# Sparse attention and two mixtures of experts on one core: drains, branch hints and fillers moved in the second mixture

## The chip, the cores and the metric

The kernel runs on one NeuronCore of a Trainium2 chip. The metric is the device time of one execution in microseconds (us), smaller is better. Three executions of the kernel before took 527.5, 528.46 and 528.85 us (median 528.46); one more was profiled and took 526.34 us.

## The reference

Three stages follow each other. Inputs are float32: 1152 tokens (2 batches of 576), width 512, eight experts of inner width 1024 in both mixtures, capacity 288 in the second.

```python
attn = softmax(mask(scale * q @ k.T)) @ v          # half the heads local, half strided
x = rows(attn)                                     # (1152, 512)

# first mixture: two experts a token, chosen by noisy logits
noisy = x @ w_gate + log1p(exp(x @ w_noise)) * noise
for each token, for its 2 best experts e, weight g:
    out[t] += g * (relu(x[t] @ w1[e]) @ w2[e])

# second mixture, on that output: one expert a token, 288 rows an expert at most
logits = x @ w_gate2;  e = argmax(logits);  g = softmax(logits)[e]
out[t] = g * (relu(x[t] @ v1[e]) @ v2[e])
```

## The kernel before, in words

The order of the work on each engine is written out by hand. PE (TensorE) multiplies; ACT and DVE empty PSUM and split float32 weights into a high part `hi` (ACT, or POOL by a CAST at L75) and a rest `lo` (DVE, L82), so that a product is three matmuls (`hi`·x high, `hi`·x low, `lo`·x high); SP loads the weights in pieces of 512 KB into six buffers `raw`; POOL issues the indirect transfers that gather and scatter rows. Three stages matter here.

**The second routing** (from L861). DVE finds the best expert of each token, PE counts ranks (L377 to L382), and `early_list(0, ...)` builds the row list of expert 0: for each of nine token tiles DVE compares (`hot`, L429) and PE sums (`place`, L435), then DVE writes the list (L439) and POOL gathers expert 0's first 128 rows (`gather`, L403). DVE then works out `bits`, a number that tells for each expert whether it has more than 128 and more than 256 rows, and all engines load it into a register (`values_load`, L900). After that PE does some matmuls whose result nobody reads (`warm`, L122; called fillers here), the second list (with a filler of 256 columns behind each of the first four tiles), and in the middle of it the four transposes of expert 0's rows (`x_cols`, L409). POOL meanwhile scatters the full list to DRAM (L500) and reads it back as `lst` (L509).

**The second mixture** (from L1061), experts 0 to 7. A pass takes 128 rows of an expert (the third one 32): `block` runs eight steps of three matmuls for the first product (two halves of four steps), then eight steps for the second. Expert e always runs `first_block`. A second and a third pass stand in `other_blocks` behind branches (`tc.If`, L1051 and L1059) that the flags decide. A branch that is taken jumps over the pass to a short stretch in which each engine raises the semaphores that the skipped instructions would have raised (EVENT_SEMAPHORE, on POOL also INC_SWDGE_SEM). In this run experts 0, 3, 5 and 6 skip both further passes, 1, 4 and 7 skip the third, and 2 runs all three.

`tell(e, b)` puts a hint on a branch into the stream of every engine: one or two register operations (L906) and a BRANCH_PREFETCH_HINT (listed at the last line of the kernel function's caller, L1166). Before, `tell(e, 1)` stands ahead of `first_block(e)` and `tell(e, 2)` at the start of the second pass.

`also(at)` is called by `block` at fixed places and holds the side work: weight splits, the transposes of the next rows, `last_rows` (the output of the expert before), `rows_ahead` (POOL gathers for the expert after next) and, at place 6, `pool.drain()` (L1032), on which POOL waits. Expert 1 at place "between" decodes `lst` on DVE (L513 to L516) and lets POOL gather expert 2's rows into the buffer that the trace calls `hot`.

Another `pool.drain()` stands in `finish` of the first mixture (L761).

```python
    def early_list(e, rk, ix, limit, busy=0, hook=None, q=1):

        for c in range(NT):
            early_hot(e, rk, limit, [c])
            early_place(c, limit)
            warm(bank[6], busy, q)
```

Of the kernel before, what the change touches and what calls it, by code (L numbers as in the profile page):

```python
# [38 lines left out]
def blocks(n):  # L39
    return [(a, min(128, n - a)) for a in range(0, n, 128)]  # L40
# [3 lines left out]
def attention_moe_moe_kernel(ctx: ExitStack, tc: tile.TileContext, a, out, capacity):  # L44
    nc = tc.nc
    pe, act, dve, pool, sp = nc.tensor, nc.scalar, nc.vector, nc.gpsimd, nc.sync
# [38 lines left out]
    def split(eng=None):  # L85
        split_lo(split_hi(), eng or dve)
# [32 lines left out]
    def warm(ps, n, q=4):  # L119

        for _ in range(n):
            pe.matmul(ps.rearrange("p (a b) -> p a b", a=4)[:, :q], ones,  # L122
                      ones[:, None, :].to_broadcast([128, q, 128]), start=True, stop=True)
# [219 lines left out]
    bank = [banks[:, i] for i in range(8)]  # L343
# [10 lines left out]
    def small(name, shape=(128, NT, E), dt=F32):  # L354
        return rt.tile(list(shape), dt, name=name)
# [18 lines left out]
    def count_ranks(sb, first, last):  # L374

        ps = bank[7][:, :(NT + 1) * E].rearrange("p (c e) -> p c e", e=E)
        pe.matmul(ps[:, :NT, :], tri, sb, start=first, stop=False, skip_group_check=True)  # L377
        pe.matmul(ps[:, NT, :], ones, sb[:, NT - 1, :], start=False, stop=False,
                  skip_group_check=True)
        for c in range(NT - 1):  # L380
            n = NT - c
            pe.matmul(ps[:, c + 1:NT + 1, :], ones, sb[:, c, None, :].to_broadcast([128, n, E]),  # L382
                      start=False, stop=last and c == NT - 2, skip_group_check=True)
        return ps

    def ranks(ps, chosen, tag):


        pen = small("pen" + tag)
        dve.tensor_scalar(pen, chosen, -BIG, BIG, op0=OP.mult, op1=OP.add)  # L390
        rk = small("rk" + tag)
        dve.tensor_tensor(rk, ps[:, :NT, :], pen, op=OP.add)
        at = small("rank" + tag)
        act.activation(at, ps[:, :NT], AF.Copy, scale=24.0)
        cnt = small("cnt" + tag, (128, E))
        act.copy(cnt, ps[:, NT])
        return rk, at, cnt
# [27 lines left out]
    def early_hot(e, rk, limit, cs=range(NT)):  # L425

        for c in cs:
            n = min(limit, 128 * (c + 1))
            dve.tensor_scalar(hot[:, c, :n], count[:, :n], rk[:, c, e:e + 1], None, op0=OP.is_equal)  # L429

    def early_place(c, limit):

        ps = bank[7][:, :3]
        for b, (s0, m) in enumerate(blocks(min(limit, 128 * (c + 1)))):
            pe.matmul(ps[:, b:b + 1], hot[:, c, s0:s0 + 128], place[:, c:c + 1],  # L435
                      start=c == 0 and b == 0, stop=c == NT - 1, skip_group_check=True)

    def early_index(ix):
        dve.tensor_scalar(ix, bank[7][:, :3], float(T), None, op0=OP.add)  # L439
# [7 lines that stand above are left out]
            if c == 6 and hook:  # L447
                hook()
        early_index(ix)
# [74 lines left out]
    def by_turns(*chains):  # L524

        chains = list(chains)
        while chains:
            chains = [c for c in chains if next(c, c) is not c]
# [330 lines left out]
    c2 = min(capacity, C1)  # L859
    nb2 = blocks(c2)  # L860
# [4 lines left out]
    rk3, at3, cnt3 = ranks(count_ranks(ohb3, True, True), oh3[:, 0], "3")  # L865
# [3 lines left out]
    h = yT.rearrange("p d s -> p (d s)")[:, :FF]  # L869
    L2 = Lists("2", oh3, at3, c2)  # L870
    early2 = [small(f"early2{i}", (128, 3), I32) for i in range(2)]
    early_list(0, rk3, early2[0], c2)
    gather(xg[0], acc, early2[0], c2, (0,))
    act.activation(d3, d3, AF.Exp)
    g3 = small("g3", (128, 1, NT))
# [2 lines left out]
    def weights2():  # L878
        dve.tensor_reduce(m3, d3, axis=AX.X, op=OP.add)
        yield  # L880
        dve.tensor_scalar(m3, m3, 1.0e-9, None, op0=OP.add)
        yield
        dve.reciprocal(g3[:, 0], m3)
        yield
        L2.weights(g3)

    def bits2():

        f = [small(f"bits{i}", (128, E)) for i in range(2)]
        for i in range(2):  # L890
            dve.scalar_tensor_tensor(f[i], cnt3, 128.0 * (i + 1), four_e, op0=OP.is_gt, op1=OP.mult)
            yield
        dve.scalar_tensor_tensor(f[0], f[1], 2.0, f[0], op0=OP.mult, op1=OP.add)
        yield
        dve.tensor_reduce(f[1][:, :1], f[0], axis=AX.X, op=OP.add)
        yield
        dve.tensor_copy(bits, f[1][:, :1])

    by_turns(weights2(), bits2(), L2.places())
    more_blocks = nc.values_load(bits[0:1, 0:1], engines=engines, min_val=0, max_val=4 ** E - 1)  # L900

    def has(e, b):
        return (more_blocks >> (2 * e + b - 1)) & 1

    def tell(e, b):
        tc.mark_branch_hint_location(f"block{e}_{b}", hint=has(e, b), engines=engines)  # L906

    pending = [split_hi() for _ in range(2)]
    early_hot(1, rk3, c2)
    warm(bank[6], 5)  # L910
    for c in range(NT):
        early_place(c, c2)
        if c < 4:
# [66 lines left out]
    def first_block(e):  # L980
        def two(n=2):
            for _ in range(n):
                if e == 0 and pending:
                    split_lo(pending.pop(0), dve)
                else:
                    split()

        def last_rows():
            put_rows(e - 1, 0, bank[0] if e % 2 else bank[7])

        def rows_ahead():
            if e + 2 < E:
                gather(xg[(e + 2) % 3], acc, L2.ix[:, e + 2], c2)

        def next_turn():
            s.append(x_turn(xg[(e + 1) % 3], 0, nb2[0][1], bank[6]))

        def also(at):
            if at == "start":
                if e:  # L1000
                    two()
                if e > 1:
                    last_rows()
                    rows_ahead()
            elif at == "up":
                if e:
                    two(1)
            elif at == "between":
                if e == 1:
                    L2.decode()  # L1010
                    gather(xg[2], acc, L2.ix[:, 2], c2)
                if e:
                    two(1)
                if len(nb2) > 1:
                    s.append(x_turn(xg[e % 3], 1, nb2[1][1], bank[5]))
                if e != 1 and e + 1 < E:
                    next_turn()
            elif at == 2:
                if len(nb2) > 1:
                    x_split(s[0], xs2, 128, nb2[1][1])  # L1020
                if e != 1 and e + 1 < E:
                    x_split(s[-1], xs2, 0, nb2[0][1])
            elif at in (3, 4, 5, 6) and e + 1 < E:
                if e == 1 and at == 6:
                    next_turn()
                    x_split(s[-1], xs2, 0, nb2[0][1])
                if e and at % 2 == 0:
                    split_lo(split_hi(on_pool=True), dve)
                else:
                    two(1)  # L1030
                if at == 6:
                    pool.drain()  # L1032
                if e == 1 and at == 4:
                    last_rows()
                if e == 1 and at == 6:
                    rows_ahead()
            elif at == 6:
                pool.drain()

        s = []  # L1040
        block(e, 0, bank[7] if e % 2 else bank[0], also)

    def other_blocks(e):

        def also(at):
            if at == "between" and len(nb2) > 2:
                x_cols(xg[e % 3], xs2, 2, nb2[2][1], ps=bank[6])

        if len(nb2) == 1:
            return  # L1050
        with tc.If(has(e, 1) > 0, preferred_fallthrough_block=True, label=f"block{e}_1"):  # L1051
            if len(nb2) > 2:
                tell(e, 2)
            if e == 0:
                L2.decode()
            block(e, 1, bank[5], also)
            put_rows(e, 1, bank[5])
            if len(nb2) > 2:
                with tc.If(has(e, 2) > 0, preferred_fallthrough_block=True, label=f"block{e}_2"):  # L1059
                    block(e, 2, bank[6], lambda at: None)  # L1060
                    put_rows(e, 2, bank[6])  # L1061

    put = []
    for e in range(E):
        if len(nb2) > 1:
            tell(e, 1)
        first_block(e)
        if e == E - 1:
            put_rows(e, 0, bank[7])
        other_blocks(e)  # L1070
# [99 lines left out]
```

## Time and profile before

| what | value |
|---|---|
| three executions | 527.5, 528.46, 528.85 us |
| profiled execution, its time | 526.34 us |
| its span, first to last instruction | 524.2 us |
| PE busy (matmuls) | 493.6 us, 94% |
| DVE, ACT, POOL busy | 300.7, 259.7, 190.0 us |
| mean granted TensorE clock | 0.974 |
| HBM traffic | 85.93 MB read, 16.26 MB written |
| second routing and second mixture | about 326 to 524 us of the span |

All times of the trace count from the first instruction. "Idle before" a row is the time that its engine stood still ahead of it, and behind the arrow stands what ended that time; an engine's name with a q is its instruction queue. [...] The profiled execution has 2.1 us outside its span.

### The profile page before, as it was taken

The page shows a single profiled execution, that of the slowest core. Times are in us where ns is not written, and L with a number is a line of the kernel's source. Part 1 is how long each engine was busy: PE and PEld are TensorE (multiplying, and loading weights), DVE is VectorE, ACT ScalarE, POOL GpSimd, SP SyncE. Part 2 cuts the span into 40 slices and gives each one's busy share as a digit, 9 for nine tenths or more (in the row PEclk, how much of TensorE's full clock was granted, in tenths as well). Part 3 has the DMA queues.
Part 4 walks back from the last instruction along what each step waited for, and adds up shares of the span by engine and source line. Part 5 has one row for each costly group of instructions (what it writes and reads, how often), then busy time and mean ns, then how long its engine had stood idle before and what let it go on. Part 6 is the DMA issues. An engine that isn't in the chain of part 4 may idle for free. (4 is left out here: it accounts for less than half of the span.)

```text
span 524.2 us, 9702 instructions
## 1 busy us (share of the span) xinstructions
PE 493.6 (94%) x3446; PEld 420.7 (80%) x3446; DVE 300.7 (57%) x664; ACT 259.7 (50%) x512; POOL 190.0 (36%) x233
## 2 busy tenths in 40 slices
PE   9999679999999999999999999797899999999896
PEld 4776559999999999999999998475677577777684
DVE  3997749565464555546555463655446048648731
ACT  4886617453544536454453532345254166457531
POOL 1444068853232150323203042682642055143300
PEclk9999859999999999999999999799999999999899
DMA  8975758789767686765747375338747049848600
GB/s 245 257 185 161 264 177 273 221 287 319 237 163 220 215 200 230 175 198 138 215 158 173 128 180 135 69 112 269 275 169 254 20 157 320 295 145 282 241 21 1
DMA packets 35742, 102.04 MB, mean 195 GB/s; under 512 B 7537, under 2 KB 8241, under 8 KB 35682
## 3 DMA queue, kind: packets, MB, share of 16 engines
q1 hardware_dynamic: 25458, 80.58, 47.1%
q0 software_dynamic: 8768, 20.43, 15.4%
q8 instruction: 34, 0.56, 0.4%
q10 hardware_dynamic: 1456, 0.27, 0.3%
q14 instruction: 26, 0.21, 0.1%
HBM read 85.93 MB, written 16.26 MB: 195 GB/s over the span
## 5 line engine op out<-in xcount | busy, mean ns | idle before, releaser
L82 DVE TENSOR_TENSOR lo<-raw,hi 128x1024 fp32r<-128x1024 f32 x128 | 156.2, 1242 | 74.8 <-ACT hi L77 67.7
L77 ACT ACTIVATE hi<-raw 128x1024 fp32r<-128x1024 f32 x116 | 120.4, 1057 | 15.4 <-PEq L1051 6.4
L592 PE MATMUL banks<-xt,hi 128*128 128x304 f32 x512 | 118.4, 311 | 0.7 <-ACT xt L418 0.4
L592 PE MATMUL banks<-ht,hi 128*128 128x304 f32 x512 | 110.1, 307 | 0.0
L592 PEld LDWEIGHTS banks<-xt,hi 128*128 128x128 f32 x512 | 87.2, 191 | 4.6 <-issue 4.0
L592 PEld LDWEIGHTS banks<-ht,hi 128*128 128x128 f32 x512 | 83.2, 188 | 0.4
L640 POOL DMA_INDIRECT acc<-rows,to x24 | 40.1, 1672 | 112.1 <-issue 78.5
L592 PE MATMUL banks<-ht,lo 128*128 128x304 f32 x256 | 77.3, 302 | 0.0
L927 PE MATMUL banks<-hi,xt 128*128 128x512 f32 (+1 forms) x208 | 68.4, 410 | 6.3 <-PEq L1051 4.0
L592 PE MATMUL banks<-xt,lo 128*128 128x304 f32 x256 | 73.7, 305 | 0.0
L927 PE MATMUL banks<-hi,ht 128*128 128x512 f32 (+1 forms) x208 | 68.6, 408 | 2.1 <-DVE ht L941 1.9
L599 ACT ACTIVATE ht<-banks 128x304 fp32r<-128x304 f32 x64 | 27.2, 425 | 55.3 <-PE banks L592 54.7
L927 PEld LDWEIGHTS banks<-hi,xt 128*128 128x128 f32 (+1 forms) x208 | 37.0, 185 | 18.2 <-issue 5.7
L592 PEld LDWEIGHTS banks<-xt,lo 128*128 128x128 f32 x256 | 49.0, 191 | 0.0
L592 PEld LDWEIGHTS banks<-ht,lo 128*128 128x128 f32 x256 | 48.2, 188 | 0.0
L600 DVE SCALAR_TENSOR_TENSOR ht<-banks,ht 128x304 fp32r<-128x304 f32 x64 | 29.9, 472 | 31.7 <-ACT ht L599 31.4
L927 PEld LDWEIGHTS banks<-hi,ht 128*128 128x128 f32 (+1 forms) x208 | 36.0, 182 | 13.1 <-DVE ht L941 5.0
L418 ACT CAST xt<-banks 128x512 fp32r<-128x512 f32 (+2 forms) x44 | 21.9, 513 | 45.0 <-PE banks L409 38.3
L419 DVE TENSOR_TENSOR xt<-banks,xt 128x512 fp32r<-128x512 f32 (+2 forms) x44 | 25.4, 591 | 29.8 <-ACT xt L418 29.8
L952 POOL DMA_INDIRECT out_dram<-rows,ix x13 | 16.0, 1227 | 71.9 <-ACT rows L947 34.5
L927 PE MATMUL banks<-lo,xt 128*128 128x512 f32 (+1 forms) x104 | 41.5, 399 | 0.0
L927 PE MATMUL banks<-lo,ht 128*128 128x512 f32 (+1 forms) x104 | 41.0, 394 | 0.0
(170 smaller groups left out, 656.3 us busy)
## 6 DMA issues: line engine op xcount, KB each, us to landing
raw<-w SPq DMA_DIRECT2D x64, 512.0 KB, 4.5
raw<-v SPq DMA_DIRECT2D x64, 512.0 KB, 4.9
acc<-zero POOLq DMA_DIRECT2D x4, 780.0 KB, 8.2
sqk<-sqk SPq DMA_DIRECT2D x4, 630.0 KB, 8.1
x_dram<-xr SPq DMA_DIRECT2D x9, 256.0 KB, 2.6
out_dram<-zero SPq DMA_DIRECT2D x3, 768.0 KB, 6.0
lv<-lv SPq DMA_DIRECT2D x4, 432.0 KB, 8.5
sv<-sv SPq DMA_DIRECT2D x4, 315.0 KB
```

The source lines that it names most:

```text
L77: act.activation(hi[i % SPLIT], raw[i % RAW], AF.Copy)
L82: eng.tensor_tensor(lo[i % SPLIT], raw[i % RAW], hi[i % SPLIT].bitcast(F32), op=OP.subtract)
L418: act.copy(h, ps[:, :, :m])
L419: dve.tensor_tensor(l, ps[:, :, :m], h.bitcast(F32), op=OP.subtract)
L592: pe.matmul(ps, w[k], x[i][:, k, :n], start=j == 0, stop=j == len(terms) - 1)
L599: act.activation(hs[0][:, f, :n], ps, AF.Relu)
L600: dve.scalar_tensor_tensor(hs[1][:, f, :n], ps, 0.0, hs[0][:, f, :n].bitcast(F32), op0=OP.max, op1=OP.subtract)
L640: i = pool.indirect_dma_start(out=acc, out_offset=bass.IndirectOffsetOnAxis(ap=L1.to[:m, e, b:b + 1], axis=0), in_=rows[e % 2][:m, b, :], ...
L927: pe.matmul(ps, stat[s], mov[x], start=first and j == 0, stop=last and j == 2)
L952: i = pool.indirect_dma_start(out=out, out_offset=bass.IndirectOffsetOnAxis(ap=L2.ix[:m, e, b:b + 1], axis=0), in_=rows[e % 2][:m, b, :DM] ...
```

## The change

Five edits, all in the second routing and mixture.

- The first list of the second routing gets a filler of 128 columns behind each of its nine tiles (`busy=1`).
- Five fillers of 512 columns now stand ahead of the load of the flags, and behind it one in place of five.
- `tell(e, 1)` moves from ahead of the expert's first pass to its place "up", which is behind the sixth of its sixteen steps.
- `tell(e, 2)` moves likewise from ahead of the second pass to its place "up".
- `pool.drain()` at place 6 goes from experts 0 to 6; expert 7 and the first mixture keep theirs.

```diff
--- before.py
+++ after.py
@@ -869,7 +869,7 @@
     h = yT.rearrange("p d s -> p (d s)")[:, :FF]
     L2 = Lists("2", oh3, at3, c2)
     early2 = [small(f"early2{i}", (128, 3), I32) for i in range(2)]
-    early_list(0, rk3, early2[0], c2)
+    early_list(0, rk3, early2[0], c2, busy=1)
     gather(xg[0], acc, early2[0], c2, (0,))
     act.activation(d3, d3, AF.Exp)
     g3 = small("g3", (128, 1, NT))
@@ -897,6 +897,7 @@
         dve.tensor_copy(bits, f[1][:, :1])
 
     by_turns(weights2(), bits2(), L2.places())
+    warm(bank[6], 5)
     more_blocks = nc.values_load(bits[0:1, 0:1], engines=engines, min_val=0, max_val=4 ** E - 1)
 
     def has(e, b):
@@ -907,7 +908,7 @@
 
     pending = [split_hi() for _ in range(2)]
     early_hot(1, rk3, c2)
-    warm(bank[6], 5)
+    warm(bank[6], 1)
     for c in range(NT):
         early_place(c, c2)
         if c < 4:
@@ -1003,6 +1004,8 @@
                     last_rows()
                     rows_ahead()
             elif at == "up":
+                if len(nb2) > 1:
+                    tell(e, 1)
                 if e:
                     two(1)
             elif at == "between":
@@ -1028,8 +1031,6 @@
                     split_lo(split_hi(on_pool=True), dve)
                 else:
                     two(1)
-                if at == 6:
-                    pool.drain()
                 if e == 1 and at == 4:
                     last_rows()
                 if e == 1 and at == 6:
@@ -1043,14 +1044,14 @@
     def other_blocks(e):
 
         def also(at):
+            if at == "up" and len(nb2) > 2:
+                tell(e, 2)
             if at == "between" and len(nb2) > 2:
                 x_cols(xg[e % 3], xs2, 2, nb2[2][1], ps=bank[6])
 
         if len(nb2) == 1:
             return
         with tc.If(has(e, 1) > 0, preferred_fallthrough_block=True, label=f"block{e}_1"):
-            if len(nb2) > 2:
-                tell(e, 2)
             if e == 0:
                 L2.decode()
             block(e, 1, bank[5], also)
@@ -1062,8 +1063,6 @@
 
     put = []
     for e in range(E):
-        if len(nb2) > 1:
-            tell(e, 1)
         first_block(e)
         if e == E - 1:
             put_rows(e, 0, bank[7])
```

On PE, where the first list ends and the flags are loaded (`hot` and `place` are the list's operands, `ones` the fillers', `bits` the flags). Before:

```order
L435 MATMUL banks<-place,hot 128x1
L122 LDWEIGHTS ones
L900 TENSOR_LOAD bits
L122 MATMUL banks<-ones 128x512
L122 LDWEIGHTS ones
```

With the change:

```order
L435 MATMUL banks<-place,hot 128x1
L122 LDWEIGHTS ones
L122 MATMUL banks<-ones 128x128
L122 LDWEIGHTS ones
L122 MATMUL banks<-ones 128x512
```

```order
L122 MATMUL banks<-ones 128x512
L122 LDWEIGHTS ones
L901 TENSOR_LOAD bits
L122 MATMUL banks<-ones 128x512
L435 LDWEIGHTS hot
L435 MATMUL banks<-place,hot 128x1
```

The flag load came right behind the list; now five wide fillers come first, and the second list follows one filler later.

On PE, from the end of expert 5 into the first pass of expert 6 (`xt` are the rows, `hi` and `lo` the weights, `yT` the first product's result). Before:

```order
L927 MATMUL banks<-lo_82,ht 32x512
L1059 UNCONDITIONAL_BRANCH x2
L1051 UNCONDITIONAL_BRANCH
L906 REGISTER_ALU x2
L1166 BRANCH_PREFETCH_HINT
L927 MATMUL banks<-hi_77,xt 128x512 x2
L927 MATMUL banks<-lo_83,xt 128x512
```

With the change, in the middle of that pass:

```order
L928 MATMUL banks<-hi_1084,xt 128x512 x2
L928 MATMUL banks<-lo_1090,xt 128x512
L907 REGISTER_ALU x2
L1165 BRANCH_PREFETCH_HINT
L939 MATMUL banks<-ident,yT 128x128 x4
L928 MATMUL banks<-hi_1085,xt 128x512 x2
```

The register operations and the hint left the start of the pass and stand ahead of the transposes behind its sixth step.

## Rows read from the trace of the kernel before

**Rows 1.** The page's 40 slices of the span: TensorE clock granted, in tenths.

```profile
PEclk9999859999999999999999999799999999999899
```

**Rows 2.** Waits of PE from 340 us to the end: us in total, times, longest.

```profile
PE banks L927 <- PEq L1051: 4.0, 4, 2.6
PE banks L927 <- DVE ht L941: 1.9, 1, 1.9
PE banks L409 <- DMA xg<-acc,early: 1.7, 1, 1.7
PE banks L927 <- ACTq L1059: 1.7, 2, 0.9
PE banks L409 <- DMA hot<-acc,ix: 1.5, 1, 1.5
```

**Rows 3.** PE in order of time, second routing: start, us, group [idle before <-releaser].

```profile
332.48 2.29 PE L122 MATMUL banks<-ones 128*128 128x512 bf16 x5 [1.74 <-DVE at L486]
...
335.79 1.09 PE L409 MATMUL banks<-ident,xg 128*128 128x128 f32 x4
...
338.28 0.49 PE L927 MATMUL banks<-hi,xt 128*128 128x512 f32 x1 [0.23 <-DVE xt L419]
```

**Rows 4.** Stretches: length, busy PE, PEld, DVE, ACT, POOL, then PEclk, DMA share, GB/s.

```profile
62.00:64.00 2.00, 1.64 (x30) 1.25 (x27) 1.59 (x9) 2.00 (x3) 0.00 (x0) 0.50 1.03 420
...
330.10:336.80 6.70, 4.96 (x39) 3.12 (x38) 3.71 (x26) 2.00 (x2) 4.53 (x9) 0.50 0.18 51
```

**Rows 5.** POOL's gather of expert 0's first rows (L403, 331 to 332.8 us).

```profile
L403 POOL DMA_INDIRECT xg<-acc,early x1: 1052/1052/1052, 331.8 to 331.8; - x1
...
DMA to landing us min/median/max: 3.3/3.3/3.3
```

**Rows 6.** List matmuls (L435), first routing with fillers, then second without: ns, first to last start.

```profile
L435 PE MATMUL banks<-place,hot x24: 163/166/187, 61.4 to 63.2; 128*128 128x1 f16 x24
...
L435 PE MATMUL banks<-place,hot x24: 163/165/187, 328.7 to 330.6; 128*128 128x1 f16 x24
```

**Rows 7.** POOL's queue: the drains of L1032, and behind expert 0's drain the semaphores.

```profile
L1032 POOLq DRAIN  x7: 2262/4261/11775, 350.9 to 488.2; - x7
...
L1051 POOLq INC_SWDGE_SEM  x1: 164/164/164, 363.2 to 363.2; - x1
```

**Rows 8.** DVE in order of time, expert 1.

```profile
358.02 0.68 DVE L941 TENSOR_TENSOR ht<-banks,ht 128x512 fp32r<-128x512 f32 x1
363.46 0.18 DVE L513 CAST ix<-lst 128x24 int32<-128x24 f32 x1 [4.76 <-DMA list<-rec,at]
```

**Rows 9.** POOL's gather of expert 2's rows (L403), and landings of all early gathers.

```profile
L403 POOL DMA_INDIRECT hot<-acc,ix x1: 1495/1495/1495, 364.4 to 364.4; - x1
...
DMA to landing us min/median/max: 4.9/4.9/4.9
...
DMA to landing us min/median/max: 3.3/3.9/8.8
```

**Rows 10.** PE in order of time at the starts of experts 6 and 7.

```profile
476.24 0.73 PE L927 MATMUL banks<-hi,xt 128*128 128x512 f32 x2 [0.47 <-PEq L1051]
...
492.37 0.72 PE L927 MATMUL banks<-hi,xt 128*128 128x512 f32 x2 [2.57 <-PEq L1051]
```

**Rows 11.** PE's queue, expert 5 into 6; last row: instruction fetches, 475.4 to 475.5.

```profile
L1051 PEldq COMPARE_BRANCH  x1: 343/343/343, 473.2 to 473.2; - x1
...
L1051 PEldq COMPARE_BRANCH  x1: 4637/4637/4637, 487.2 to 487.2; - x1
...
L1051 PEldq EVENT_SEMAPHORE  x1: 51/51/51, 475.8 to 475.8; - x1
...
L1166 PEldq BRANCH_PREFETCH_HINT  x1: 30/30/30, 476.2 to 476.2; - x1
...
q8 instruction: 1, 0.02, 64.0%
```

**Rows 12.** The stretch behind expert 6's late branch (columns as in rows 4).

```profile
493.87:497.28 3.41, 3.41 (x10) 2.64 (x9) 2.36 (x2) 1.31 (x4) 1.41 (x1) 0.50 0.34 133
```

## The prediction, as put on record before the changed kernel ran

> **What bounds the kernel now.** I began with the clock line of the page: PE's clock is granted in full but for three places, near 60, 330 and 490 us [rows 1]; the change touches the last two. Then I read PE's waits from the second mixture on. PE is busy there almost without a break; its idle time from 340 us to the end comes in five kinds, 10.8 us in all [rows 2]: 4.0 behind branches of L1051, 1.9 behind DVE's L941, 1.7 and 1.5 behind two gathers, and 1.7 where ACT's queue at L1059 comes last. Whatever of it goes, the end comes earlier by as much, as long as nothing else grows late. So each edit is priced by the PE gap that it can close.
>
> **Fillers in the first list: 0.** Nine fillers of 128 columns stand between the list's 24 matmuls. DVE paces that list. In the first routing the same list has the same nine fillers, at the lower clock, and runs from 61.4 to 63.2 us; without them, in the second routing, from 328.7 to 330.6 us [rows 6]. So they hide under DVE: 1.8 us with them at half rate, 1.9 us without. If they stood in the way one by one, at the list's own pace (1.9 us by 24, 0.08 us each), the gather behind the list would start 0.7 us later; that end I keep.
>
> **Fillers ahead of the flags: 1.1 us.** Before, PE waits 1.74 us for the flags, and only then runs five fillers, which take 2.29 us at the lower clock; its four transposes of expert 0's rows start at 335.79 and take 1.09 us [rows 3]. The clock is at 0.50 from 330.1 to 336.8 us [rows 4]. With the change the five run in that wait, and behind the flags there is one: even at the lower clock four fifths of 2.29 us, 1.8 us, leave the way to the transposes. They cannot go that early, since their rows are late next: the gather starts at 331.8 and lands 3.3 us later, at 335.1 [rows 5]. So the transposes start 0.7 us earlier. PE was busy with 512-column fillers ahead of the place where the clock rose; now such work begins 1.7 us sooner, so I expect the upper level when they run. At twice the rate they take about 0.6 us instead of 1.09, and 0.4 us more is gained. ACT and DVE follow, and the second product waits for DVE's L419 at 338.28 [rows 3]. Gain 1.1 us, ends 0.4 (late list, lower clock) and 1.2. POOL's chain of scatters and all of expert 0 move along.
>
> **Drains: 2.4 us, all of it at expert 0's drain.** Seven drains go, of 2.3 to 11.8 us [rows 7]. The first is the long one: from 350.9 for 11.8 us, to 362.7. Behind it in POOL's queue stands expert 0's taken branch, and there POOL raises the semaphores of what was skipped, at 363.2 [rows 7]. DVE is done with L941 at 358.7 and stands until 363.46 ahead of L513 [rows 8]. The trace puts that wait down to the list's transfer, but it ends just as POOL's semaphore instruction does, so I take POOL as its cause. Queued behind L513 on DVE are a weight split and the next L941, for which PE idles 1.9 us [rows 2]; POOL's gather of expert 2's rows starts at 364.4, behind DVE's decode, lands 4.9 us later [rows 9], and PE idles another 1.5 us for it [rows 2]. Without the drain POOL's semaphores come behind its last gather, long before 358, DVE decodes at once, and the 1.9 us go. The gather then starts some 4.8 us earlier, but PE also comes 1.9 us earlier, and weight loads fill the queues then: it may take from 4.9 to the 8.8 us of the slowest early gather [rows 9]. With 4.9 the wait of 1.5 us is gone, with 8.8 it is 1.5 + 1.9 + 3.9 - 4.8 = 2.5. I take 1.0, as most early gathers are nearer the low end. So 1.9 + 0.5 = 2.4 us, ends 0.9 and 3.4. The other six drains I cost at nothing: no wait of PE names POOL [rows 2], and the gathers behind them are for the expert after next. The cover is PE's own work, 16 us from the start of expert 6 to that of expert 7 [rows 10], against a median drain of 4.3 us [rows 7]; were it gone, the drains would show as waits of PE for a gather, and there are only the two early ones.
>
> **Hints: 0.8 us, and expert 6's branch, 3.8 us.** Two register operations and the hint stood in each gap between experts. A normal gap is 0.47 us [rows 10]; from the semaphore of the jump at 475.8 [rows 11] to the first matmul at 476.24 PE's queue issues four instructions in some 0.4 us, and three of them are these: about 0.28 us. In the middle of a pass they are issued while matmuls are queued, and cost nothing. The gap goes down where PE's own queue ends it: at the starts of experts 1, 4, 6 and 7. At expert 1 the gain is lost in the wait for the early gather (1.7 us) [rows 2]; where ACT's queue comes last [rows 2] it is not there either. Three times 0.28 is 0.8 us.
>
> Expert 6's branch is another matter. PE's taken branch of expert 5 took 0.343 us, expert 6's 4.637 [rows 11], and the gap ahead of expert 7 is 2.57 us instead of 0.47 [rows 10]: 2.1 us. Behind it the clock stood at 0.50 for 3.41 us of unbroken matmuls [rows 12], which loses half of that, 1.7 us. So this branch costs 3.8 us. Why this one? Its hint was issued at 476.2; an instruction fetch had begun between 475.4 and 475.5, and its share, 64% of 16 engines over 0.1 us, makes it 1.02 us long [rows 11]. So the hint fell into a running fetch, which I take to have swallowed it. The fetch followed expert 5's jump. From that hint to the branch at 487.2 PE's queue went through sixteen steps in 11.0 us, 0.69 us each. Now the hint comes six steps later, 4.1 us, clear of that fetch, and still 6.9 us ahead of the branch, more than the 4.6 us that a missed target cost. I expect a branch of about 0.35 us. Ends: nothing (the stall stays) and 3.8 us.
>
> **The sum.** 1.1 + 2.4 + 0.8 + 3.8 = 8.1 us off the profiled 526.34 us is 518.2. The median of the shown runs lies 2.1 us above the profiled execution, so on it 528.46 - 8.1 = 520.4 us.
>
> **Rivals.**
> *The page of instructions decides, not the hint.* The drains and fillers help, but expert 6's branch, or another of the seven that are taken, stalls as before: PE's program is now twenty instructions longer ahead of the mixture, so every jump lands elsewhere in its fetched pieces. For it: I saw one case only of a hint inside a fetch. Against it: four jumps go over the same two passes, and only the one with that hint was late; the other three share 1.4 of the 4.0 us [rows 2]. Time 528.46 - 4.3 = 524.2 us. [...]
>
> *The drain is not what DVE waits for.* If POOL's semaphore instruction itself waits for the gathers in flight, it comes little earlier without a drain, and most of the 2.4 us stays: 528.46 - 5.7 = 522.8 us. For it: 11.8 us of drain are far more than POOL needs to issue a gather (1.05 and 1.5 us) [rows 5, 9], so POOL can be held until transfers are through. Against it: the semaphore instruction itself took 0.16 us [rows 7].
>
> *Hints too late, slower than before.* If a hint behind the sixth step no longer gets its page in time, all seven taken branches of PE stall as expert 6's does, six more than before, each 2.1 us of gap, and clock on top where the level falls (1.7 us each). Six times 2.1 is 12.6 us; less the 4.3 us of fillers, drains and shorter gaps that leaves 8.3 us more: 536.8 us. It decides from where the time from hint to branch falls under 4.6 us; above it came out at 6.9 us, which speaks against it.
>
> *Fillers do nothing.* In the first routing the clock was 0.50 from 62 to 64 us, under such fillers [rows 4]. That takes only the 0.4 us of the clock.
>
> **How the numbers follow.** Chances: the forecast 0.55 (520.4, from 518 to 522.5); a stall stays or comes elsewhere 0.25 (524.2); the drains give little 0.08 (522.8); two stalls, so about no change, 0.07 (528); hints late 0.05 (536.8). The range from 517.5 to 525.5 takes in the first three and their bounds and leaves out some 0.15. No change means within 0.3% (about what a measurement of this kernel can tell), 526.9 to 530.0: 0.09. Faster 0.85, slower 0.06.
>
> **What would show it.** Right: no DRAIN at L1032's place in experts 0 to 6; DVE's L513 right behind L941; PE's wait for L941 gone; the gap ahead of expert 7 near 0.2 us and the clock at 1.00 there; transposes of expert 0 at about 335. Wrong: a COMPARE_BRANCH of 4 us on PE anywhere, a DVE wait of over 1 us ahead of L513, or a wait for `hot` that grew beyond 2.5 us.

## The result and the profile after

The changed kernel took 522.21 us (median of 6, 520.99 to 524.0), the kernel before 528.65 (median of 6, 526.0 to 531.3): a ratio of 0.989, 95% interval 0.9847 to 0.9934. The forecast was 520.4, range 517.5 to 525.5. Set beside the kernel before once more, with more executions, it came to 0.9947 (0.9912 to 0.9982; 524.38 against 527.86). So it is faster, by 6.4 us in the first comparison and 3.5 in the second; what both intervals share is 0.9912 to 0.9934, 3.5 to 4.6 us, where 8.1 were forecast. The profiled execution of the changed kernel took 522.86 us with a span of 520.9.

Its lines are numbered one to three higher than those of before: L927 became L928, L941 L942, L1051 L1054, L1059 L1060. The page's clock line:

```profile
PEclk9999959999999999999999999989999999999999
```

The dip near 330 us is now near 340, and the one near 490 is gone [rows 1]. The upper level is a granted clock of 1.00 in the trace, the lower one of 0.50. PE's waits from 340 us to the end, as in [rows 2]:

```profile
PE banks L928 <- PEq L1054: 2.0, 1, 2.0
PE banks L409 <- DMA hot<-acc,ix: 1.8, 1, 1.8
PE banks L928 <- ACTq L1060: 1.6, 2, 0.8
PE banks L928 <- DVE ht L942: 1.2, 3, 0.7
```

6.6 us in place of 10.8. The wait for the early gather is gone, and three of the four behind the branches. The fourth, ahead of expert 7, is still there. PE's queue at L1054, expert 5's branch and then expert 6's:

```profile
L1054 PEldq COMPARE_BRANCH  x1: 344/344/344, 472.2 to 472.2; - x1
...
L1054 PEldq COMPARE_BRANCH  x1: 4362/4362/4362, 486.1 to 486.1; - x1
```

The hint of that branch now stood at 477.19 us, clear of the instruction fetch that began at 474.10, and the branch was as late as before [rows 11]: the gap is 2.05 us, against 2.57 [rows 10]. PE in order of time at the start of expert 7, and the clock there:

```profile
490.67 0.71 PE L928 MATMUL banks<-hi,xt 128*128 128x512 f32 x2 [2.05 <-PEq L1054]
```

```profile
491.00:497.28 6.28, 6.28 (x33) 5.15 (x32) 5.52 (x6) 4.61 (x7) 1.25 (x1) 1.00 0.45 165
```

The level did not fall this time behind the gap [rows 12]. In the second routing it fell later than before. PE in order of time behind the flags [rows 3], then two stretches [rows 4]:

```profile
333.33 0.38 PE L122 MATMUL banks<-ones 128*128 128x512 bf16 x1 [0.58 <-DVE at L486]
...
336.20 0.98 PE L409 MATMUL banks<-ident,xg 128*128 128x128 f32 x4 [1.44 <-DMA xg<-acc,early]
```

```profile
330.10:336.30 6.20, 4.17 (x51) 2.45 (x52) 4.60 (x30) 2.00 (x2) 4.19 (x9) 1.00 0.30 64
336.38:343.20 6.82, 6.44 (x28) 4.89 (x28) 1.89 (x3) 2.49 (x3) 5.18 (x10) 0.50 0.48 146
```

The fillers ran at the upper level (1.00), then PE stood 1.44 us for the rows, and it was expert 0's first products that ran at 0.50. In the second profile of the changed kernel (after_again below) the transposes still ran at the upper level, and the level fell right behind them, for 3.41 us. PE's transposes there, then the stretches before and behind the fall:

```profile
335.36 0.66 PE L409 MATMUL banks<-ident,xg 128*128 128x128 f32 x4 [1.19 <-DMA xg<-acc,early]
```

```profile
333.20:336.50 3.30, 1.90 (x34) 1.59 (x31) 1.59 (x8) 1.98 (x3) 2.31 (x4) 1.00 0.30 81
336.55:339.96 3.41, 3.27 (x7) 2.35 (x8) 1.90 (x3) 1.99 (x3) 2.85 (x4) 0.50 0.55 98
```

At expert 0's drain, POOL's queue, DVE in order of time, and POOL's gather of expert 2's rows [rows 7 to 9]:

```profile
L1054 POOLq INC_SWDGE_SEM  x1: 573/573/573, 352.0 to 352.0; - x1
```

```profile
360.73 0.68 DVE L942 TENSOR_TENSOR ht<-banks,ht 128x512 fp32r<-128x512 f32 x1
361.33 0.17 DVE L513 CAST ix<-lst 128x24 int32<-128x24 f32 x1
```

```profile
L403 POOL DMA_INDIRECT hot<-acc,ix x3: 870/944/1528, 362.3 to 365.3; - x3
...
DMA to landing us min/median/max: 6.4/6.4/6.4
```

POOL's semaphores came at 352 instead of 363, and L513 stands right behind L942.

**Where the time went.** For each kernel I took the first product of an expert (the first matmul of the products' line that reads `xt` behind a taken branch) and the time from one to the next, in profiled executions. Experts 2 and 4 hardly vary (37.7 and 27.1 us, but for 28.2 in page_plus_104) and are left out. "Flags" is the load of the flags on PE (L900, 332.13 us before); "expert 7" runs to the end.

```
                          flags to
                          expert 1  expert 1  expert 3  expert 5  expert 6  expert 7
before                      19.59     32.50     13.58     13.69     16.13     31.86
changed kernel              20.81     29.67     13.26     13.37     15.69     30.27
changed kernel, again       19.33     28.02     13.26     13.36     16.13     30.31
page_plus_48                20.22     29.52     13.25     13.37     13.81     31.90
page_plus_104               19.05     28.66     16.63     15.85     15.10     30.80
no_hints                    20.74     29.76     13.26     13.37     13.81     31.82
hint6_out                   23.14     28.05     13.26     13.38     13.80     31.79
before_no_hints             23.44     28.35     13.25     13.36     13.81     31.78
drains_out_no_hints         24.09     27.38     13.25     13.36     13.83     31.83
after_minus_hints           21.98     27.75     13.26     13.37     13.80     31.81
drains_alone                26.80     26.68     13.58     13.69     15.90     31.86
hints_alone                 23.42     28.14     13.25     13.37     15.52     31.87
fillers_alone               27.23     27.01     13.57     13.69     15.74     31.85
drains_and_hints            22.17     27.44     13.25     13.37     16.19     31.86
```

Between the first two rows lie +1.22, -2.83, -0.32, -0.32, -0.44 and -1.59: 4.3 us less. The +1.22 is a net: expert 0's first product came 0.55 us earlier behind the flags (4.87 against 5.42), and the lower clock in its products cost more than that. In the second profile of the changed kernel the same column is 0.26 us shorter than before. (The routing started later in the profile after, flags at 332.99 us against 332.13, which gives back 0.9 of the 4.3; the list's first matmul already stood that much later, and nothing ahead of it was changed.) The table is used below.

### The profile page after: what moved, and what is told of

It is laid out like the page before. It is cut to its first block, busy times and chain, and to the rows that moved or that the text cites. A ratio compares the mean times of both kernels' runs of the same rounds, so it can differ in the third digit from the quotient of the medians.

```text
span 520.9 us, 9715 instructions
## 1 busy us (share of the span) xinstructions
PE 493.0 (95%) x3456; PEld 420.3 (81%) x3456; DVE 300.8 (58%) x664; ACT 259.5 (50%) x512; POOL 189.3 (36%) x233
## 5 line engine op out<-in xcount | busy, mean ns | idle before, releaser
L928 PE MATMUL banks<-hi,xt 128*128 128x512 f32 (+1 forms) x208 | 68.9, 412 | 4.5 <-PEq L1054 2.0
L928 PE MATMUL banks<-hi,ht 128*128 128x512 f32 (+1 forms) x208 | 68.6, 409 | 1.2 <-DVE ht L942 1.2
L599 ACT ACTIVATE ht<-banks 128x304 fp32r<-128x304 f32 x64 | 27.1, 423 | 55.0 <-PE banks L592 54.4
L928 PEld LDWEIGHTS banks<-hi,xt 128*128 128x128 f32 (+1 forms) x208 | 37.5, 188 | 16.6 <-issue 4.1
L928 PEld LDWEIGHTS banks<-hi,ht 128*128 128x128 f32 (+1 forms) x208 | 36.1, 182 | 12.3 <-DVE ht L942 4.2
L942 DVE TENSOR_TENSOR ht<-banks,ht 128x512 fp32r<-128x512 f32 (+1 forms) x26 | 17.1, 659 | 43.0 <-ACT ht L941 42.9
L928 PE MATMUL banks<-lo,xt 128*128 128x512 f32 (+1 forms) x104 | 41.8, 402 | 0.0
```

The source lines that it names most:

```text
L599: act.activation(hs[0][:, f, :n], ps, AF.Relu)
L928: pe.matmul(ps, stat[s], mov[x], start=first and j == 0, stop=last and j == 2)
L942: dve.tensor_tensor(hl, ps, hh.bitcast(F32), op=OP.subtract)
```

## The experiments

Ratios are to the kernel before on the same chip, with 95% intervals; kernels of one group ran on one chip.

### The parts one by one

**drains_alone**: before, without these lines.

```diff
-                if at == 6:
-                    pool.drain()
```

> The kernel before with the seven drains of the second mixture gone and nothing else. The prediction's sum says 2.4 us faster (0.9 to 3.4): DVE's L513 right behind L941 at expert 0, PE's wait for L941 (1.9 us) gone, the wait for hot at most 1.0; expert 6's branch still 4.6 us. If POOL's semaphore instruction waits for its transfers without a drain too, at most 0.5 us faster. If the six later drains cost something as well, more than 3.4 us.

Measured: 525.83 us against 525.84, ratio 0.9991 (0.9963 to 1.0019). No gain. The three signs at expert 0 are there (L513 right behind L941, no wait of PE for L941, none for `hot`), and nothing came of it.

**hints_alone**: before, with the `tell` calls at `"up"`.

```diff
             elif at == "up":
+                if len(nb2) > 1:
+                    tell(e, 1)
...
-        if len(nb2) > 1:
-            tell(e, 1)
         first_block(e)
```

> The kernel before with the hints moved behind a block's sixth step and nothing else. If the place of the hint decides over expert 6's branch: 4.6 us faster (0.8 of shorter gaps, 3.8 of the branch). If the place of the branch in PE's program decides, as the changed kernel's trace suggests: expert 6's branch stays at about 4.5 us and only the gaps of experts 1, 4, 6 and 7 shrink, 0.8 to 1.1 us faster.

Measured: ratio 0.9988 (0.9959 to 1.0017). Expert 6's branch took 4.26 us. Experts 3 and 5 became 0.33 and 0.32 us shorter in the table, so the shorter gaps are real, too small for this measurement. The run also shows why drains_alone had nothing to gain. It keeps the drains; POOL's queue at the drain's line, and DVE at the start of expert 1:

```profile
L1034 POOLq DRAIN  x2: 6287/6297/6307, 352.6 to 368.8; - x2
```

```profile
363.40 0.68 DVE L941 TENSOR_TENSOR ht<-banks,ht 128x512 fp32r<-128x512 f32 x1
364.00 0.17 DVE L513 CAST ix<-lst 128x24 int32<-128x24 f32 x1
```

Expert 0's drain took 6.3 us and ended at 358.9, 5.1 us ahead of L513, which waits for nothing. In the profiled execution of before it took 11.8 us and ended 4.0 behind the end of L941 [rows 7, 8].

**fillers_alone**: before, with the three filler edits.

```diff
-    early_list(0, rk3, early2[0], c2)
+    early_list(0, rk3, early2[0], c2, busy=1)
...
+    warm(bank[6], 5)
     more_blocks = nc.values_load(...)
...
-    warm(bank[6], 5)
+    warm(bank[6], 1)
```

> The kernel before with the fillers of the second routing moved and nothing else. The prediction's term: 1.1 us faster (0.4 to 1.2). The rival, from the changed kernel's trace, where the clock was at 0.50 from 336.4 to 343.2 us, in expert 0's products, and not in the routing: the rows come 0.4 us earlier, but about 3.4 us of work at the upper level is lost, so 2 to 3 us slower; if such a fall only moves the rest of the mixture to a time when it waits less, 0 to 1 us slower.

Measured: ratio 1.0025 (0.9986 to 1.0065), by the medians 3 us slower: no gain, perhaps a loss. The stretch behind the routing:

```profile
336.10:342.80 6.70, 6.32 (x27) 4.87 (x28) 1.90 (x3) 2.49 (x3) 5.01 (x10) 0.50 0.44 125
```

Again expert 0's products ran at 0.50.

**drains_and_hints**: the two diffs of drains_alone and hints_alone together; the fillers as before:

```diff
-    early_list(0, rk3, early2[0], c2, busy=1)
+    early_list(0, rk3, early2[0], c2)
...
-    warm(bank[6], 5)
     more_blocks = nc.values_load(...)
...
-    warm(bank[6], 1)
+    warm(bank[6], 5)
```

This diff is against the changed kernel.

> The changed kernel without its fillers: drains gone and hints moved. By the prediction's terms with expert 6's stall kept: 3.2 us faster than before, so 1 us or more slower than the changed kernel (6.4 us faster than before). If the fillers cost time by the clock in expert 0: 7 to 9 us faster than before, faster than the changed kernel; the clock at 1.00 from 337 to 350 us.

Measured: ratio 0.9966 (0.9935 to 0.9997), 1.8 us by that ratio. The clock is at 0.50 in the routing and not behind it:

```profile
330.00:337.00 7.00, 5.20 (x44) 3.19 (x45) 4.64 (x30) 2.00 (x2) 4.71 (x11) 0.50 0.25 55
337.00:347.00 10.00, 9.37 (x58) 7.62 (x57) 2.66 (x4) 4.27 (x6) 7.36 (x14) 0.99 0.36 106
```

That looks as if moving the fillers moved the fall into the products, but the other kernels with the fillers as before show that it is not that simple. In hints_alone the level was at 0.50 in the routing and in expert 0's first products too:

```profile
332.20:339.02 6.82, 4.70 (x39) 2.92 (x37) 3.45 (x25) 2.65 (x4) 4.51 (x9) 0.50 0.23 68
339.02:342.40 3.38, 3.38 (x7) 2.44 (x8) 1.97 (x3) 1.85 (x2) 2.00 (x3) 0.50 0.22 41
```

Of six profiles with the fillers as before, four have 3.4 to 3.6 us of these products at 0.50 and two (before, drains_and_hints) none; of eight with the fillers moved, all have 3.2 to 6.5 us. So with the fillers moved it came every time, and in four of the eight for 4.9 us or more; what decides in a single execution is open.

On this chip drains and hints together gained much less than 6.4 us; the whole did not run on it. All four profiles here hold a pause of PE that neither profile from the first comparison has: 2.0 to 3.6 us in expert 0's last steps, while the second half of `ht` comes late out of ACT's L940. In drains_alone, ACT in order of time:

```profile
354.48 0.58 ACT L940 CAST ht<-banks 128x512 fp32r<-128x512 f32 x1 [6.39 <-remote]
```

It began 4.4 us after the end of the transposes that it waits for; in before it stood 2.05 us, and PE's transposes released it. "flags to expert 1" is longer for it, and expert 1, whose rows then have landed, shorter. With expert 0 late by itself, neither the drain nor the early gather is on the path; that fits, but no profile of before on this chip was taken to show it.

### What makes expert 6's branch late

I counted PE's instructions in the program: 8,712 before and 8,732 now. The trace has 34 instruction fetches of 16 KB on queue q8 (0.56 MB), before and now, which is one for about 256 of them. In my count, which starts at the program's first instruction, expert 6's branch stands at place 163 of a piece of 256 before and at 183 now; where the borders of the fetched pieces lie in this count, no run shows exactly.

**after_again**: the changed kernel, same chip as the next three.

> The changed kernel as it is, beside the kernel before on one chip in more rounds. If the gain is the kernel's: 5 to 7 us faster than before again (ratio 0.987 to 0.991). If a good part of the first 6.4 us was the scatter of executions, as the parts alone (drains 0, hints 0, fillers 1 us slower, drains and hints 1.8 us faster) suggest: 1 to 3 us faster.

Measured: ratio 0.9947 (0.9912 to 0.9982). Between the two guesses. Its profiled execution, 519.46 us, has the late branch too (4.86 us, gap 2.47), and again no fall of the clock behind it.

**page_plus_48** and **page_plus_104**: the eight fillers ahead of the second routing cut up, which only moves PE's later instructions.

```diff
-    warm(bank[6], 8)
+    warm(bank[6], 32, 1)
```

```diff
-    warm(bank[6], 8)
+    warm(bank[6], 4, 1)
+    for _ in range(56):
+        pe.matmul(bank[6][:, :64], ones, ones[:, :64], start=True, stop=True)
```

> The changed kernel with the eight fillers of 512 columns ahead of the second routing cut into 32 of 128: the same columns, but 48 instructions more in PE's program ahead of all the mixture's jumps. Theory of the border: PE's program is fetched in pieces of 256 instructions, and a jump is late where it goes into the piece behind the next border and stands within some 50 instructions behind the last one; expert 6's branch then stands 75 or more behind it, as expert 0's does, which was on time. It takes about 0.35 us, the gap ahead of expert 7 is 0.2 to 0.5 us, and the kernel is 1.5 to 4 us faster than the changed kernel. Theory of the second long jump in a row, and any theory of the hint: expert 6's branch stays at 4.3 us or more, no change.

> The same with 104 instructions more (4 fillers of 128 columns and 56 of 64, the same columns). Theory of the border: now the branches of experts 3 and 5 stand where expert 6's stood, 35 and 19 instructions behind a border with their targets behind the next: both take 4 us or more, expert 6's about 0.35 us; one more gap of 2 us than in the changed kernel, 2 to 4 us slower. Second long jump in a row or the hint: only expert 6's stays late, no change.

Measured: 0.9887 (0.9837 to 0.9937) and 1.0026 (0.9992 to 1.0061), that is, by the medians, 2.7 us faster and 4.4 slower than the changed kernel. In the second the branches of experts 3 and 5 are late, expert 6's is not:

```profile
L1056 PEldq COMPARE_BRANCH  x1: 5917/5917/5917, 429.6 to 429.6; - x1
...
L1056 PEldq COMPARE_BRANCH  x1: 5048/5048/5048, 474.5 to 474.5; - x1
...
L1056 PEldq COMPARE_BRANCH  x1: 337/337/337, 492.1 to 492.1; - x1
```

In the first, expert 6's still took 2.44 us where 0.35 was expected (a fetch had begun with it), short enough that PE, with products queued, had a gap of 0.15 us only:

```profile
L1054 PEldq COMPARE_BRANCH  x1: 2440/2440/2440, 486.3 to 486.3; - x1
```

So the place in PE's program decides *which* of the branches with a hint is late; the theory of the "second long jump in a row" falls.

**no_hints**: the changed kernel without hints for the blocks, and the eight fillers cut into 16 of 256 columns, so that the branches stand within 14 instructions of their places.

```diff
-    warm(bank[6], 8)
+    warm(bank[6], 16, 2)
+    warm(bank[6], 0, 1)
...
             elif at == "up":
-                if len(nb2) > 1:
-                    tell(e, 1)
...
-            if at == "up" and len(nb2) > 2:
-                tell(e, 2)
```

> The changed kernel without any hint for the blocks' branches, eight fillers of 512 columns cut into 16 of 256 so that the branches stand within 14 instructions of their places in the changed kernel. If hints bring the target in time: the other taken branches of PE stall as expert 6's does, 2 us of gap each, 10 us or more slower. If only the place against the border counts: expert 6's branch alone is late, all others 0.2 to 0.37 us as before, and the time stays within 1 us of the changed kernel.

Measured: ratio 0.9885 (0.9852 to 0.9918), 1.9 us faster than the changed kernel by the medians. Neither expectation held. No branch is late, expert 6's neither:

```profile
L1051 PEldq COMPARE_BRANCH  x1: 342/342/342, 488.6 to 488.6; - x1
```

That left two theories: the 10 to 11 instructions by which this branch had moved, or the hint itself. The next group, on a chip of its own, tells them apart.

**hint6_out**: the changed kernel without the one hint for expert 6.

```diff
-                if len(nb2) > 1:
+                if len(nb2) > 1 and e != 6:
                     tell(e, 1)
```

**before_no_hints**: before, without the blocks' hints, `warm(bank[6], 8)` cut so that branch and target stand where the changed kernel has them (183; target 167 for 168).

```diff
-    warm(bank[6], 8)
+    warm(bank[6], 30, 1)
+    warm(bank[6], 1, 2)
...
-            if len(nb2) > 2:
-                tell(e, 2)
...
-        if len(nb2) > 1:
-            tell(e, 1)
         first_block(e)
```

> The changed kernel without the one hint for expert 6's first branch, on all engines; PE's branch and its target move by three instructions. If that branch's own hint makes it late: about 0.34 us in place of 4.4 to 4.9, no gap of 2 us, 2 to 4 us faster than the changed kernel (519 to 522 us where before takes 527). If its place against a border alone decides, or the hints ahead of it: 4 us or more again, no change.

> The kernel before without the blocks' hints, its drains and fillers kept (eight fillers of 512 columns cut into 30 of 128 and one of 256, so that expert 6's branch and target stand exactly where the changed kernel has them, 183 and 167 in a piece of 256). If the hint makes the branch late: 0.34 us there, and 3 to 5 us faster than before (the gap of 2.1, the clock's 1.7, and 0.3 in each gap between experts). If the place decides: 4 us or more at that branch, at most 1 us faster.

Measured: 0.9959 (0.993 to 0.9987) and 0.9961 (0.9935 to 0.9986), 3.0 and 2.7 us faster than before by the medians (3 to 5 were expected of the second). Expert 6's branch, first in the one, then in the other:

```profile
L1054 PEldq COMPARE_BRANCH  x1: 348/348/348, 485.9 to 485.9; - x1
```

```profile
L1052 PEldq COMPARE_BRANCH  x1: 345/345/345, 488.4 to 488.4; - x1
```

One hint taken out, the eleven others that run in the mixture kept: on time. Same place, no hints: on time. So **the hint makes this branch late**. It takes a hint and a place: every branch of 4 us and more had a hint, stood at 163 to 183 in my count by 256, and jumped over two passes. Place and hint alone are not enough: two branches over one pass, each with a hint, were on time at such places (expert 7's at 163 in the changed kernel, 0.34 us; expert 4's at 172 in page_plus_104, 0.24). Nor is the 2.44 us of page_plus_48 explained by its place, 231, where expert 0's branch in the changed kernel took 0.37. All other taken branches of PE took 0.17 to 0.46 us, with a hint or without one.

A fetch came with the hint and without it. In every late branch a fetch of 16 KB started while the branch waited, and the branch ended 1.35 to 1.51 us behind that fetch's end (in the profile after the fetch ended at 489.08 us, the branch at 490.43). In hint6_out a fetch came as well, from 488.85 to 489.95 us, but its branch had ended at 486.24, 2.6 us ahead of it. What links the hint to that wait no run shows.

It is worth less than its gap. In the table expert 6 shrinks from 15.5 to 16.2 us to 13.8, but expert 7 is then never under 31.7: PE comes 2 us earlier and waits for DVE. In no_hints, PE in order of time, expert 7:

```profile
499.50 0.49 PE L929 MATMUL banks<-hi,ht 128*128 128x512 f32 x1 [1.22 <-DVE ht L943]
```

Experts 6 and 7 together take 48.0 us before (late, and the clock falls behind it; 47.4 to 48.0 in the other kernels with both), 46.0 and 46.4 in the changed kernel (late, no fall), 45.6 without the late branch.

**drains_out_no_hints**: before_no_hints without the drains.

```diff
-                if at == 6:
-                    pool.drain()
```

> The same without the seven drains too; the fillers are the kernel before's. Against the run before it this shows the drains alone, clear of the late branch: the prediction's term is 2.4 us (0.9 to 3.4); drains alone on the kernel before gave 0 to 2. Against the run with the changed kernel's fillers and no hints (0.9885 of before) it shows the fillers: 1 us better with them by the prediction, 0 to 2 us worse by the clock at 0.50 behind the routing.

Measured: ratio 0.9979 (0.9948 to 1.001), by the medians 2.2 us *slower* than with the drains; the intervals overlap, so no gain from taking the drains out and no sure loss. In before_no_hints, which keeps them, the drain at expert 0 (6.5 us, to 359.4) had ended long before DVE came to L513 (364.52). For the fillers, no_hints ran on another chip and can't be set beside it. hint6_out can: it has the fillers moved, no drains and eleven hints in mid-pass, and was 2.5 us faster by the medians, with intervals that overlap. It is level with before_no_hints, which has the fillers and the drains as before (522.24 and 522.54 us): on this chip fillers and drains, taken together, made no difference that these times can show.

**after_minus_hints**: the changed kernel less its hints, nothing else, on a fourth chip.

```diff
-                if len(nb2) > 1:
-                    tell(e, 1)
...
-            if at == "up" and len(nb2) > 2:
-                tell(e, 2)
```

> The changed kernel with the blocks' hints taken out and nothing else changed. If a hint only ever costs here: all taken branches of PE at 0.17 to 0.37 us, PE's idle time by its own queue ahead of an expert below 0.3 us everywhere, 5 to 6 us faster than before (0.9885 as the run without hints). If that earlier run owed half of it to its chip: 2 to 3 us faster (0.995).

Measured: ratio 0.9961 (0.9934 to 0.9988). No late branch; PE's waits from 340 us:

```profile
PE banks L928 <- DVE ht L942: 1.9, 4, 1.2
PE banks L928 <- ACTq L1056: 1.6, 2, 0.8
PE banks L928 <- ACT ht L941: 1.2, 1, 1.2
PE banks L409 <- DMA hot<-acc,ix: 0.6, 1, 0.6
PE banks L928 <- PEq L1050: 0.4, 1, 0.4
```

The pause in expert 0 is here as well (1.2 us), and the gain, 2.9 us by the medians, is the smaller one that was expected. Without hints the changed kernel is ahead of before on both chips, and of the changed kernel where they ran together (0.9885 and 0.9947), though there the two intervals still overlap. No version that ran is clearly better; page_plus_48 (0.9887) on the one chip, and hint6_out and before_no_hints on another, are level with it.

## Why the prediction came out as it did

The time lay within the range and on the forecast side; the sum got there partly by other terms than it named. One of its own signs of being wrong, a branch of 4 us on PE, is in the profile. The rival in which a stall stays had 4.3 us off, which lies in the 3.5 to 4.6 that the two comparisons share; that the first median came within 2 us of the forecast owes something to the scatter of executions, as the second comparison gave 3.5.

- **Fillers in the first list, 0: right.** From the first to the last of the list's matmuls it took 1.84 us before and 1.83 after, and the flags came 3.41 and 3.39 us behind the first. The gather's issue, 3.02 us behind it before, came at 3.27 and 2.92 in the two profiles after.
- **Fillers ahead of the flags, 1.1: right up to the first product, lost behind it.** The transposes started 0.44 and 0.64 us earlier from the flags (3.65 before, 3.21 and 3.01), bound by the rows as the text had it (forecast 0.7). "I expect the upper level when they run" held in six of the eight profiles with moved fillers, at 0.66 us (forecast about 0.6); in the profile after and in fillers_alone the level fell with them (0.98 and 1.12). The first product came 0.55 and 1.08 us earlier behind the flags in the two profiles of the changed kernel. What failed is "all of expert 0 move along": the level then stood at 0.50 in expert 0's products, for 5.4 us of them in the profile after and 3.3 in the second. From the flags to expert 1 the profiled pair lost 1.2 us, the second profile won 0.3, and alone the fillers gained nothing (1.0025). The prediction's rival "fillers do nothing" was too kind: it did not ask where the level would fall next.
- **Drains, 2.4: the mechanism was right, its size was that of one execution.** Without the drain DVE passes L513 at once, the 1.9 us go, and with them the wait for the early gather that the sum had left out (1.7); the wait for `hot` stays at 1.8 (0.7 in the second profile), as the text feared with its upper end. Expert 1 became 2.8 and 4.5 us shorter in the two profiles of the changed kernel. But 11.8 us was a long drain: in the three other profiles with drains it took 4.7 to 6.5 us and was over before DVE needed it, and the drains taken out alone gave 0.9991. The step that failed is to take that one wait as the kernel's. In the profile of before the last early gather landed at 361.90 us, 0.8 ahead of the drain's end, so the drain seems to follow the landings; the other three show none to compare. No run took out the drains where they were long, so their share in the gain rests on the traces alone. The six others at nothing agrees: experts 2 to 5 and 7 show no change from drains.
- **Hints in gaps, 0.8: right in size.** 0.32 us at each of the starts of experts 4 and 6 (0.28 forecast), in every kernel with the hints moved or gone. At expert 7 the late branch covers it.
- **Expert 6's branch, 3.8: wrong.** "So the hint fell into a running fetch, which I take to have swallowed it": in the profile after the hint was clear of any fetch and 8.9 us ahead of its branch (6.9 forecast), and the branch took 4.36 us all the same. hint6_out (0.35 us) shows the opposite of a lost hint, a hint that holds the branch up. How it does so no run shows. Nor does one show that the 4.6 us were the cost of a missed target, or that a hint has to get a page in time: the late branches ended 1.35 to 1.51 us behind the end of a fetch, and hint6_out's 2.6 us ahead of the start of one. The rival that a stall stays was right about the stall, and half right about the cause: the place in PE's pieces picks the branch, but without a hint that place is harmless (0.35 us at 183 in before_no_hints). The size was off too: with its clock the late branch cost 2.4 us in experts 6 and 7 (48.0 against 45.6), not 3.8, because PE waits for DVE when it comes earlier (1.2 in no_hints). Of those 2.4 the profiled pair got 2.0 with the branch still late, as the clock did not fall; why it did not is open.

## What to carry to other kernels

Price a wait from several executions before you count on it: a drain of 11.8 us here took 4.7 to 6.5 in other profiles, and the wait behind it was not there. Before you move fillers, ask where the clock may fall next, and whether real products then stand in it: here, with the fillers moved, 3.2 to 6.5 us of products ran at 0.50 in all eight profiles. And test a prefetch hint by leaving it out: here each cost 0.3 us in a gap that PE's own queue ended, no branch was late without them, and one made its branch 4 us late.

## What the runs showed that I had not expected

- A branch with a hint can be slower than one without: 4.26 to 5.92 us against 0.34 at like places.
- The kernel before had medians of 525.2 to 528.7 us in the five comparisons, and single executions of 521.6 to 531.3: terms under 2 us can be seen in a profile's gaps, but not in these times.
- On three of the chips PE paused 1.2 to 3.6 us in expert 0, in all eight profiles taken there; in the other six profiles it never did. What holds ACT's L940, whose transposes were done, is not settled. No gain on those three was over 3.0 us by the medians, the others reached 6.4; that the one follows from the other was not tried.
- POOL's semaphore instruction at an expert's first branch took 0.57 to 1.1 us in the profile after, without a drain ahead of it (L1054), and 0.16 to 0.17 before, with one (L1051) [rows 7]; no wait of PE names it.
